# Rational FFN after bucketed attention: both parts of the quotient made on the vector engine

## The chip, the cores and the metric

The kernel runs on one core of one Trainium2 chip. The time is device microseconds of one execution; the run of before was made three times: 946.79, 947.19 and 948.58 us, median 947.19 us. The profile is that of one more execution, which took 947.28 us.

## The reference

An attention over 32 heads of 768 positions, in which a query sees only the keys of its own hash bucket, is followed by a feed-forward layer with a rational activation. Only the second part is touched by the change:

```python
def _moe_ref(x, w_in, w_out, a, b):          # x: 3072 x 512, d_ff 2048
    h = x @ w_in
    h2 = h * h
    h3 = h2 * h
    P = a[0] + a[1] * h + a[2] * h2 + a[3] * h3
    Q = 1.0 + np.abs(b[0]) * np.abs(h) + np.abs(b[1]) * h2
    g = P / (Q + 1e-06)
    return (g @ w_out).astype(np.float32)
```

All of it is float32.

## The kernel before

The attention takes the first 400 us or so. The FFN works on blocks of 384 tokens (8 of them, number t) and chunks of 128 of the 2048 hidden features (16, number f), so on 128 steps (t, f), counted through as i = 0 to 127. The kernel calls TensorE PE, the vector engine DVE, ScalarE ACT and GpSimd POOL, as the profile does.

Float32 products are made from parts: a number is split into a high part in the format fp32r (tiles xh, wi_hi, gh) and the remainder (xl, wi_lo, gl), and three products of parts are summed. So a step has twelve matmuls for h (`Gemm1`, line 581; tile psh; 4 chunks of 128 input features times 3 products) and nine for the output sum (`gemm2`, line 680; tile pso; 3 groups of 128 tokens times 3 products: gh twice, gl once).

`Ffn.step(i)` (line 696) writes the order of the work by hand; each engine keeps its instructions in program order. In one call:

- the first product of step i, and `terms(i)` (line 647): three ACT operations (square, |b0 h|, a3 h + a2) and three on DVE. They leave w = Q - 1 and c, the numerator without a0, in tile `w` (3 buffers) and tile `c1` (3 buffers; the profile shows it as c);
- `quotient(i-1)` (line 660): ACT makes r = 1/Q as exp(-ln Q); DVE makes w = (w + 1.000001) r, then c = (c + a0) r, then c = (w - 2) c. The last two factors are a Newton step on the reciprocal; the result is -g. Tile `r` has 2 buffers;
- `parts(i-2)` (line 673): ACT copies -g to gh, rounded to fp32r, and POOL subtracts: gl = -g - gh. Both have 4 buffers;
- `gemm2(i-4)`: the LAG of 4 steps (line 634) lies between a chunk's first product and its use in the second. At f = 15 ACT copies the three sums out with the factor -1, and they are stored.

During block t the next block's tokens are loaded (`Tokens.load`, line 607). In each of the first 7 blocks this puts four operations of 128 x 768 on DVE (two products x, two remainders xl) and two on ACT, after the steps f = 6, 7, 8 and 12, 13, 14. At i = 6 DVE also makes the last reciprocals of the attention (`recips`). The product of a step lies in one of four PSUM buffers, so PE can be at most four first products ahead of DVE's last reader.

All instructions are issued through a helper, so the profile gives them all as line L88; the tiles tell them apart.

Of the kernel before, what the change touches and what calls it, by code (L numbers as in the profile page):

```python
# [7 lines left out]
F32 = mybir.dt.float32  # L8
F32R = mybir.dt.float32r
# [3 lines left out]
AF = mybir.ActivationFunctionType  # L13
ALU = mybir.AluOpType
# [616 lines left out]
class Ffn:  # L631
# [28 lines left out]
    def quotient(self, t, f):  # L660

        nc = self.nc
        a0, a1, a2, a3, b0, absb1, qbias = self.coef
        w, p = self.state[t, f]
        r = self.tile("r", t, f)
        nc.scalar.activation(r, w, AF.Ln, bias=qbias)
        nc.scalar.activation(r, r, AF.Exp, scale=-1.0)
        nc.vector.scalar_tensor_tensor(out=w, in0=w, scalar=1.0 + 1e-6, in1=r, op0=ALU.add, op1=ALU.mult)
        nc.vector.scalar_tensor_tensor(out=p, in0=p, scalar=a0, in1=r, op0=ALU.add, op1=ALU.mult)
        nc.vector.scalar_tensor_tensor(out=p, in0=w, scalar=2.0, in1=p, op0=ALU.subtract, op1=ALU.mult)  # L670
        self.state[t, f] = p

    def parts(self, t, f):
        p = self.state[t, f]
        gh, gl = self.tile("gh", t, f, 4, F32R), self.tile("gl", t, f, 4, F32R)
        self.nc.scalar.copy(gh, p)
        self.nc.gpsimd.tensor_tensor(out=gl, in0=p, in1=gh.bitcast(F32), op=ALU.subtract)
        self.state[t, f] = gh, gl

    def gemm2(self, t, f):  # L680
        nc = self.nc
        gh, gl = self.state.pop((t, f))
        for i in range(NTK // P):
            if f == 0:
                self.sums[t, i] = self.ps_o.tile([P, DM], F32, tag="pso", name=f"pso{t}_{i}")
            ps = self.sums[t, i]
            ts = slice(i * P, i * P + P)
            for n, (g, w) in enumerate(((gh, 0), (gh, 1), (gl, 0))):
                nc.tensor.matmul(ps, g[:, ts], self.wo[f][:, w, :], start=(f == 0 and n == 0), stop=(f == NFC - 1 and n == 2))
            if f == NFC - 1:  # L690
                o = self.tp.tile([P, DM], F32, tag="o", name=f"o{t}_{i}", bufs=3)
                nc.scalar.activation(o, ps, AF.Identity, scale=-1.0)
                r0 = t * NTK + i * P
                nc.sync.dma_start(self.out[r0 : r0 + P, :], o)

    def step(self, i):
        seq = [(t, f) for t in range(NBLK) for f in range(NFC)]
        if i < len(seq):
            self.gemm(*seq[i])
            self.terms(*seq[i])  # L700
        if 0 <= i - 1 < len(seq):
            self.quotient(*seq[i - 1])
        if 0 <= i - 2 < len(seq):
            self.parts(*seq[i - 2])
        if i >= self.LAG:
            self.gemm2(*seq[i - self.LAG])
        self.done = i + 1
# [70 lines left out]
```

## Time and profile before

| | us |
|---|---|
| median of the three runs | 947.19 |
| the profiled execution | 947.28 |
| its span, from the first to the last instruction | 945.5 |
| PE busy in the span | 937.1 |
| DVE busy | 863.1 |
| ACT busy | 679.7 |
| POOL busy | 454.7 |

How it is read: the page gives each engine's busy time and a strip of 40 slices; the groups of instructions give the mean duration of each kind; the waits name who waited for whom; the timeline gives every instruction's start and duration. Instructions of one engine overlap by some 0.08 us in the records when the second does not need the result of the first: the next one starts before the one ahead has ended. So the sum of durations is more than the time taken, and what an operation takes of DVE's time is read as the distance from its start to the next start.

### The profile page before, as it was taken

The page shows a single profiled execution, that of the slowest core. Times are in us where ns is not written, and L with a number is a line of the kernel's source. Part 1 is how long each engine was busy: PE and PEld are TensorE (multiplying, and loading weights), DVE is VectorE, ACT ScalarE, POOL GpSimd, SP SyncE. Part 2 cuts the span into 40 slices and gives each one's busy share as a digit, 9 for nine tenths or more (in the row PEclk, how much of TensorE's full clock was granted, in tenths as well). Part 3 has the DMA queues.
Part 4 walks back from the last instruction along what each step waited for, and adds up shares of the span by engine and source line. Part 5 has one row for each costly group of instructions (what it writes and reads, how often), then busy time and mean ns, then how long its engine had stood idle before and what let it go on. Part 6 is the DMA issues. An engine that isn't in the chain of part 4 may idle for free.

```text
span 945.5 us, 14855 instructions
## 1 busy us (share of the span) xinstructions
PE 937.1 (99%) x5062; PEld 750.6 (79%) x5062; DVE 863.1 (91%) x1206; ACT 679.7 (72%) x1420; POOL 454.7 (48%) x403
## 2 busy tenths in 40 slices
PE   8999999999999999999999999999999999999998
PEld 4666666666666666589989999899899899998996
DVE  6799889888988896599999999999999999999996
ACT  7577767676767666787777777777777777777775
POOL 5587878787878777832222222222222222222222
PEclk9999999999999999999999999999999999999999
DMA  6677877788777767357021011021010110210000
GB/s 212 193 197 211 235 213 234 215 222 224 233 217 229 220 192 219 117 205 246 6 68 34 1 67 35 1 67 35 32 48 22 63 39 1 67 34 1 34 1 34
DMA packets 49888, 111.65 MB, mean 118 GB/s; under 512 B 9138, under 2 KB 21798, under 8 KB 49812
## 3 DMA queue, kind: packets, MB, share of 16 engines
q1 hardware_dynamic: 49524, 110.60, 39.6%
q8 instruction: 40, 0.66, 0.3%
q14 instruction: 36, 0.29, 0.1%
q10 hardware_dynamic: 288, 0.10, 0.0%
HBM read 56.82 MB, written 21.17 MB: 82 GB/s over the span
## 4 chain that ended last, share of the span: by engine, by line
PE 92%; DVE 5%; DMA 1%; issue 1%; ACT 0%; SPq 0%; DVEq 0%; ACTq 0%
PE psh L88 28%; PE pso L88 28%; PE pss L88 14%; PE psv L88 12%; PE psm L88 6%; DVE m L88 3%; PE psu L88 2%; PE psb L88 1%; DVE ws L88 1%; DMA wr<-w_in 1%; DMA kf<-kT 0%; DVE c L88 0%; DVE wr L88 0%; DVE lo L88 0%; DVE rd L88 0%
## 5 line engine op out<-in xcount | busy, mean ns | idle before, releaser
L88 POOL TENSOR_TENSOR gl<-c,gh 128x384 fp32r<-128x384 f32 x128 | 141.4, 1105 | 393.4 <-ACT gh L88 369.4
L88 ACT ACTIVATE E<-pss 128x384 f32<-128x384 f32 x384 | 167.8, 492 | 112.0 <-PE pss L88 97.5
L88 PE MATMUL pso<-wo,gh 128*128 128x512 f32 x768 | 241.1, 395 | 0.0
L88 DVE TENSOR_REDUCE m<-psm 128x1 f32<-128x768 f32 x192 | 179.4, 948 | 34.6 <-PE psm L88 31.4
L88 POOL TENSOR_TENSOR acc<-E,E 128x384 f32<-128x384 f32 x128 | 160.6, 1273 | 85.7 <-ACT E L88 85.4
L88 PE MATMUL pss<-q,k 128*128 128x384 f32 (+2 forms) x768 | 172.8, 348 | 1.1 <-ACT E L88 0.7
L88 PE MATMUL psh<-xl,wi_hi 128*128 128x384 f32 x512 | 172.1, 336 | 0.0
L88 PE MATMUL psh<-xh,wi_hi 128*128 128x384 f32 x512 | 171.7, 335 | 0.0
L88 PE MATMUL psh<-xh,wi_lo 128*128 128x384 f32 x512 | 171.5, 335 | 0.0
L88 PEld LDWEIGHTS pso<-wo,gh 128*128 128x128 f32 x768 | 142.9, 188 | 23.8
L88 PEld LDWEIGHTS pss<-q,k 128*128 128x128 f32 (+2 forms) x768 | 133.9, 189 | 33.2 <-issue 20.1
L88 PE MATMUL pso<-wo,gl 128*128 128x512 f32 x384 | 152.1, 396 | 0.3 <-POOL gl L88 0.3
L88 ACT ACTIVATE h<-psh 128x384 f32<-128x384 f32 x128 | 63.0, 492 | 123.2 <-PE psh L88 123.2
L88 DVE SCALAR_TENSOR_TENSOR c<-c,ab,r 128x384 f32<-128x384 f32 x128 | 145.9, 1140 | 0.0
L88 POOL TENSOR_TENSOR acc<-acc,E 128x384 f32<-128x384 f32 x128 | 142.6, 1133 | 2.3 <-ACT E L88 2.3
L88 PE MATMUL psv<-E,v 128*64 128x385 f32 x768 | 133.0, 492 | 0.0
L88 PE MATMUL psm<-k,q 76*128 76x384 f32 (+1 forms) x384 | 102.1, 349 | 2.0 <-DVE m L88 1.0
L88 PEld LDWEIGHTS psv<-E,v 128*64 128x64 f32 x768 | 51.9, 136 | 65.0 <-issue 63.7
L88 PEld LDWEIGHTS psh<-xh,wi_hi 128*128 128x128 f32 x512 | 96.1, 188 | 6.3 <-issue 1.2
L88 PEld LDWEIGHTS psh<-xl,wi_hi 128*128 128x128 f32 x512 | 96.0, 188 | 5.1
L88 PEld LDWEIGHTS psh<-xh,wi_lo 128*128 128x128 f32 x512 | 96.1, 188 | 0.0
L88 ACT ACTIVATE c<-psh,ab 128x384 f32<-128x384 f32 x128 | 86.7, 677 | 1.6 <-POOL gl L88 1.4
(77 smaller groups left out, 1284.5 us busy)
## 6 DMA issues: line engine op xcount, KB each, us to landing
q<-q SPq DMA_DIRECT2D x45, 192.0 KB
k<-k SPq DMA_DIRECT2D x45, 192.0 KB
wr<-w_in SPq DMA_DIRECT2D x16, 512.0 KB
wr<-w_out SPq DMA_DIRECT2D x16, 512.0 KB
wo_d<-wr SPq DMA_DIRECT2D x16, 512.0 KB
wo<-wo_d SPq DMA_DIRECT2D x16, 512.0 KB
qf<-qT SPq DMA_DIRECT2D x16, 384.0 KB
kf<-kT SPq DMA_DIRECT2D x16, 384.0 KB
```

The lines of the kernel that those rows point to most:

```text
L88: return self.tc.keep_in_program_order(issue(*args, **kwargs))
```

## The change

The quotient's high part is now DVE's own product gh = (c + a0) r, written as fp32r. The rest of the division is formed from it: w = (w + 1.000001) gh, that is Q times gh, then c = (c + a0) - w, and the low part is gl = c r. `parts` is gone, and with it ACT's copy and POOL's subtraction; DVE has four operations in `quotient` where it had three. The sign is now that of g, so the output copy has no factor.

```diff
         r = self.tile("r", t, f)
+        gh, gl = self.tile("gh", t, f, 4, F32R), self.tile("gl", t, f, 4, F32R)
         nc.scalar.activation(r, w, AF.Ln, bias=qbias)
         nc.scalar.activation(r, r, AF.Exp, scale=-1.0)
-        nc.vector.scalar_tensor_tensor(out=w, in0=w, scalar=1.0 + 1e-6, in1=r, op0=ALU.add, op1=ALU.mult)
-        nc.vector.scalar_tensor_tensor(out=p, in0=p, scalar=a0, in1=r, op0=ALU.add, op1=ALU.mult)
-        nc.vector.scalar_tensor_tensor(out=p, in0=w, scalar=2.0, in1=p, op0=ALU.subtract, op1=ALU.mult)
-        self.state[t, f] = p
-
-    def parts(self, t, f):
-        p = self.state[t, f]
-        gh, gl = self.tile("gh", t, f, 4, F32R), self.tile("gl", t, f, 4, F32R)
-        self.nc.scalar.copy(gh, p)
-        self.nc.gpsimd.tensor_tensor(out=gl, in0=p, in1=gh.bitcast(F32), op=ALU.subtract)
+        nc.vector.scalar_tensor_tensor(out=gh, in0=p, scalar=a0, in1=r, op0=ALU.add, op1=ALU.mult)
+        nc.vector.scalar_tensor_tensor(out=w, in0=w, scalar=1.0 + 1e-6, in1=gh.bitcast(F32), op0=ALU.add, op1=ALU.mult)
+        nc.vector.scalar_tensor_tensor(out=p, in0=p, scalar=a0, in1=w, op0=ALU.add, op1=ALU.subtract)
+        nc.vector.tensor_tensor(out=gl, in0=p, in1=r, op=ALU.mult)
         self.state[t, f] = gh, gl
...
-                nc.scalar.activation(o, ps, AF.Identity, scale=-1.0)
+                nc.scalar.copy(o, ps)
...
-        if 0 <= i - 2 < len(seq):
-            self.parts(*seq[i - 2])
```

What this does to DVE's queue, in the rows of the built programs: c is the numerator tile, psh the first product in PSUM, ab the coefficients, h the square; the first number behind a name is f, and the brackets name the engines whose semaphores the instruction waits for. Before, quotient of step 4 and then the terms of step 6:

```order
L88 SCALAR_TENSOR_TENSOR w_4_4886<-w_4_4886,r_4_4939 128x384 [waits Activation_49]
L88 SCALAR_TENSOR_TENSOR c_4_4887<-c_4_4887,ab,r_4_4939 128x384
L88 SCALAR_TENSOR_TENSOR c_4_4887<-w_4_4886,c_4_4887 128x384 [waits DVE_49]
L88 SCALAR_TENSOR_TENSOR w_6_4973<-h_6_4972,absb_85,w_6_4973 128x384 [waits Activation_49]
L88 TENSOR_TENSOR c_6_4974<-psh_6_4959,c_6_4974 128x384 [waits Activation_49]
L88 SCALAR_TENSOR_TENSOR c_6_4974<-c_6_4974,ab,psh_6_4959 128x384 [waits DVE_49]
```

After, the same place of DVE's queue:

```order
L88 SCALAR_TENSOR_TENSOR gh_4_4940<-c_4_4888,ab,r_4_4939 128x384 [waits PE_49,Activation_49]
L88 SCALAR_TENSOR_TENSOR w_4_4887<-w_4_4887,gh_4_4940 128x384 [waits DVE_49]
L88 SCALAR_TENSOR_TENSOR c_4_4888<-c_4_4888,ab,w_4_4887 128x384 [waits DVE_49]
L88 TENSOR_TENSOR gl_4_4941<-c_4_4888,r_4_4939 128x384 [waits DVE_49,PE_49]
L88 SCALAR_TENSOR_TENSOR w_6_4972<-h_6_4971,absb_85,w_6_4972 128x384 [waits Activation_49]
L88 TENSOR_TENSOR c_6_4973<-psh_6_4958,c_6_4973 128x384 [waits Activation_49]
L88 SCALAR_TENSOR_TENSOR c_6_4973<-c_6_4973,ab,psh_6_4958 128x384 [waits DVE_49]
```

Three of the four operations now wait for the operation right ahead of them on the same engine (DVE_49), where one of three did; and gh and gl each carry a second wait, for PE's last reading of the buffer that they write (from f = 4 of the first block on, 124 steps). In the built program an instruction holds one wait; the first of two stands in an instruction of its own ahead, which does nothing but wait.

## The prediction

> **What bounds the kernel now.** I read the page first, then the waits from 480 us on, then windows, and last the timeline of DVE. The busy shares of the page and its strip for DVE (40 slices of the span):
>
> ```profile
> PE 937.1 (99%) x5062; PEld 750.6 (79%) x5062; DVE 863.1 (91%) x1206; ACT 679.7 (72%) x1420; POOL 454.7 (48%) x403
> DVE  6799889888988896599999999999999999999996
> ```
>
> PE is busy all the time, but in the FFN (the right half of the strip) DVE shows nines as well. The waits after 480 us, as who waited for whom, us in total, times, longest, and the windows of the FFN:
>
> ```profile
> ACT h L88 <- PE psh L88: 103.1, 93, 1.2
> PE pso L88 <- POOL gl L88: 0.3, 1, 0.3
> 404.00:560.00 156.00, 156.00 (x797) 140.55 (x796) 150.91 (x243) 120.04 (x242) 40.93 (x37) 1.00 0.28 95
> 560.00:760.00 200.00, 200.00 (x1004) 180.67 (x1003) 195.63 (x299) 149.14 (x302) 53.63 (x48) 1.00 0.12 36
> ```
>
> PE (the second number of a window) has no gap, at a granted clock of 1.00; its only wait is 0.3 us at the very end. ACT waits for PE. So PE bounds the FFN, and its step is read from ACT's square of the product, once per step; between these two rows lie 55 steps:
>
> ```profile
> 700.01 0.49 ACT L88 ACTIVATE h<-psh 128x384 f32<-128x384 f32 x1 [0.47 <-PE psh L88]
> 930.64 0.49 ACT L88 ACTIVATE h<-psh 128x384 f32<-128x384 f32 x1 [1.21 <-PE psh L88]
> ```
>
> That is 230.63 / 55 = 4.19 us per step. Taking work off ACT and POOL can therefore gain only the 0.3 us at the end. What matters is DVE, of which the change asks more. How much of its 4.19 us does it need? Start, duration, operation:
>
> ```profile
> 708.67 0.61 DVE L88 SCALAR_TENSOR_TENSOR c<-c,ab,r 128x384 f32<-128x384 f32 x1
> 709.32 0.56 DVE L88 SCALAR_TENSOR_TENSOR c<-w,c 128x384 f32<-128x384 f32 x1
> 709.79 0.61 DVE L88 SCALAR_TENSOR_TENSOR w<-h,absb,w 128x384 f32<-128x384 f32 x1
> 710.32 0.55 DVE L88 TENSOR_TENSOR c<-psh,c 128x384 f32<-128x384 f32 x1
> 710.91 0.61 DVE L88 SCALAR_TENSOR_TENSOR c<-c,ab,psh 128x384 f32<-128x384 f32 x1
> 711.44 0.55 DVE L88 SCALAR_TENSOR_TENSOR w<-w,r 128x384 f32<-128x384 f32 x1
> 711.91 1.38 DVE L88 SCALAR_TENSOR_TENSOR c<-c,ab,r 128x384 f32<-128x384 f32 x1
> 713.32 0.56 DVE L88 SCALAR_TENSOR_TENSOR c<-w,c 128x384 f32<-128x384 f32 x1
> 711.52 1.35 POOL L88 TENSOR_TENSOR gl<-c,gh 128x384 fp32r<-128x384 f32 x1 [3.18 <-ACT gh L88]
> ```
>
> From start to start, the terms take 0.53, 0.59 and 0.53 (709.79 to 711.44, 1.65), the quotient 0.47 (711.44 to 711.91), 0.65 (708.67 to 709.32) and 0.47 (709.32 to 709.79): 3.24 us. The operation that lies beside POOL's subtraction took 1.38 where its like took 0.61: it ends 0.42 after POOL does, as if it had been held. So 0.76 of DVE's "busy" time is waiting behind POOL, and DVE has room of almost 1 us per step. Two kinds of distance stand here. Where the next operation does not need the result, it starts 0.08 before the end (709.32 + 0.56 = 709.88, next at 709.79). Where it does (708.67 + 0.61 = 709.28, next at 709.32; 710.32 + 0.55 = 710.87, next at 710.91), it starts 0.04 behind the end. A dependence thus costs some 0.12.
>
> **The change part by part.** Gone: ACT's copy, POOL's subtraction, and with POOL the hold.
>
> ```profile
> L88 ACT CAST gh<-c 128x384 fp32r<-128x384 f32 x91 | 45.3, 498 | 0.0
> L88 DVE TENSOR_TENSOR x<-x,r 128x768 f32<-128x768 f32 x11 | 10.5, 951 | 0.0
> L88 DVE TENSOR_TENSOR xl<-x,xh 128x768 fp32r<-128x768 f32 x11 | 10.5, 951 | 0.0
> ```
>
> The copy's 0.50 us on ACT lay beside PE, which ACT waits for anyway: worth nothing. That gh is written as fp32r costs DVE nothing: xl and x take the same 951 ns. The output copy without its factor stays on ACT, three times per block beside PE: taken as nothing, at most a tenth of its time once, at the end.
>
> DVE's quotient, each operation waiting for the one ahead: gh 0.64 to 0.65, as its like above (0.61 and 0.04; I take 0.64, which the one quoted further down has); w, with a constant instead of a column, 0.55 + 0.04 = 0.59; c again 0.64; gl is followed by an operation that does not need it, 0.47 (as c<-w,c; 0.53 if it is like the forms with a column). Sum 2.34. With the terms 3.99 us per step, without the second waits.
>
> The second wait of gl is the unknown. Its first wait, for DVE's own result, moves into an instruction of its own, so behind the end of c come two steps instead of one. Before has such a pair on DVE, at the end of the attention:
>
> ```order
> L88 SCALAR_TENSOR_TENSOR ws_4637<-ws_4637,wr_4636 128x512 [waits DVE_49]
> L88 ISA ws_4637<-wr_4636,ws_4637 128x1024 [waits DVE_49,Activation_49]
> L88 TENSOR_TENSOR wr_4636<-ws_4637,wr_4636 128x512 [waits Activation_49]
> L88 SCALAR_TENSOR_TENSOR w_0_4711<-h_0_4710,absb_85,w_0_4711 128x384 [waits PE_49,Activation_49]
> L88 TENSOR_TENSOR c_0_4712<-psh_0_4697,c_0_4712 128x384 [waits Activation_49]
> ```
>
> The second row is that operation; ISA there is the custom operation of the profile. ACT has one in the last step, whose copy to gh waits for DVE and PE, while the copy before it waits for DVE alone:
>
> ```profile
> 401.48 1.37 DVE L88 SCALAR_TENSOR_TENSOR ws<-ws,wr 128x512 int32<-128x512 int32 x1
> 402.98 1.28 DVE L88 CUSTOM_DVE_ANT_0 ws<-wr,ws 128x1024 uint16<-128x1024 uint16 x1
> 410.14 0.61 DVE L88 SCALAR_TENSOR_TENSOR c<-c,ab,r 128x384 f32<-128x384 f32 x1
> 410.78 0.56 DVE L88 SCALAR_TENSOR_TENSOR c<-w,c 128x384 f32<-128x384 f32 x1
> 935.23 0.56 DVE L88 SCALAR_TENSOR_TENSOR c<-w,c 128x384 f32<-128x384 f32 x1
> 935.82 0.51 ACT L88 CAST gh<-c 128x384 fp32r<-128x384 f32 x1 [1.12 <-DVE c L88]
> 936.82 1.25 DVE L88 SCALAR_TENSOR_TENSOR c<-w,c 128x384 f32<-128x384 f32 x1
> 938.16 0.51 ACT L88 CAST gh<-c 128x384 fp32r<-128x384 f32 x1 [1.82 <-DVE c L88]
> ```
>
> On DVE 402.98 - 402.85 = 0.13 behind the end, against 0.03 with one wait (410.78 - 410.75): 0.10 more, but the operation is a custom one. On ACT 0.09 (938.16 - 938.07) against 0.03: 0.06 more. I take 0.07, nearer to the plain operation, with 0 and 0.10 as ends. The second wait of gh I take at nothing: gh does not need the operation right ahead of it, so its wait for PE, long over, is passed while that one runs; 0.06 if it isn't. What is queued behind gl on DVE is the next step's terms, and for those wait ACT's ln and then PE, four steps on.
>
> Now the sum. The steps i = 0 to 3 have no second products yet (the LAG), so PE takes about half a step's time for each of them and DVE falls behind at once; with 3.99 + 0.07 per step and the tokens (0.87 four times per block of 16) it needs 4.28 where PE needs 4.19, and cannot catch up. So DVE has no idle time, and its own work sets the end. The rows for the start, the reciprocals at i = 6, and a remainder with the operation behind it:
>
> ```profile
> 405.90 0.62 DVE L88 SCALAR_TENSOR_TENSOR w<-h,absb,w 128x384 f32<-128x384 f32 x1 [0.25 <-ACT w L88]
> 407.98 0.62 DVE L88 SCALAR_TENSOR_TENSOR w<-h,absb,w 128x384 f32<-128x384 f32 x1 [0.31 <-ACT w L88]
> 429.40 0.18 DVE L88 TENSOR_SCALAR rz<-rs 128x48 f32<-128x48 f32 x1
> 430.56 0.90 DVE L88 TENSOR_TENSOR x<-x,r 128x768 f32<-128x768 f32 x1
> 705.41 0.95 DVE L88 TENSOR_TENSOR xl<-x,xh 128x768 fp32r<-128x768 f32 x1
> 706.27 0.61 DVE L88 SCALAR_TENSOR_TENSOR w<-h,absb,w 128x384 f32<-128x384 f32 x1
> ```
>
> 405.90 start; 0.43 idle until 407.98 (behind terms of 1.65); 128 x 1.65 = 211.2; 128 x 2.34 = 299.5; 124 x 0.07 = 8.7; 28 token operations x 0.87 = 24.4 (705.41 to 706.27, with 0.95 - 0.08); reciprocals 1.16. DVE is through at 951.3, and gl's own end is 0.08 later, 951.4. Behind it PE has seven of the last step's nine matmuls. The end of before:
>
> ```profile
> 937.71 0.50 PE L88 MATMUL pso<-wo,gl 128*128 128x512 f32 x1 [0.32 <-POOL gl L88]
> 941.38 0.40 PE L88 MATMUL pso<-wo,gl 128*128 128x512 f32 x1
> ```
>
> From the one to the end of the other lie 16 matmuls, 4.07 us, so seven take 1.78: 953.2. From the last matmul's end to the end of the span there were 945.5 - 941.78 = 3.72 us: 956.9, or 11.4 more than the 945.5 now. On the profiled 947.28 this is 958.7; that execution lies 0.1 over the median, so 947.19 + 11.4 = **958.6 us**.
>
> The point from which it decides: gl of the last step must be there by 941.78 - 1.78 = 940.0, so DVE may take (940.0 - 0.1 - 405.9 - 0.4 - 24.4 - 1.2) / 128 = 3.97 us per step, waits and all. My 3.99 + 0.07 is 2% over it, and all 128 steps pay.
>
> **The rivals.**
>
> *The second wait is free* (the sequencer passes both at once): 8.7 less, 949.9 us, +0.3%. For it: the operation's other wait is long over. Against it: both pairs of rows above.
>
> *DVE keeps up, and nothing changes or a little is gained.* If a wait cost nothing and only the pipe's flow counted, the operations would follow each other at 0.53 (four with a column) and 0.47 (three without): 3.53 us per step, far under 3.97; PE would stay the bound, and without its 0.3 us wait the time is 946.9. The mechanism is that of the rows at 709.32 and 709.79. Against it are the rows at 708.67 and 709.32 in the same step: the dependent one comes 0.04 behind the end. [...]
>
> *gh's second wait shows too*, at ACT's 0.06 in 124 steps: 7.4 more, 966.0. Against it: the operation ahead of gh runs 0.61, time enough to pass a wait that is over. With gl's at the custom operation's 0.10 alone it would be 3.7 more, 962.3, which I count with the forecast.
>
> **How the numbers follow.** Forecast 0.72 (DVE bound, second wait of gl between 0.05 and 0.10, each step good to 0.02, which is 2.5 us: 954 to 963); free wait 0.10; DVE keeps up 0.08; gh's wait shows too 0.10. The range from 949.5 to 963 holds the first two, 0.82. A measurement here can tell some 0.2% from no change, 1.9 us, so 945.3 to 949.1 is "same". Slower: forecast, free wait and gh's wait, less a little of the free wait that may fall under 949.1: 0.90. Of the 0.08, most is same, 0.07, and faster 0.03 allows for a gain that I don't see.
>
> **What would show it.** Right: in the timeline of DVE no idle time in the FFN; c<-c,ab,r and w<-w,r never beyond 0.65; behind c some 0.10 to gl; a step from 4.06 us without tokens; PE waiting for gl by DVE, some 11 us in all, most of it in blocks 2 to 7 and a few us in the last steps, where PE has only second products left and DVE is still more than two steps behind. Wrong: DVE waiting for ACT's w in every step (then it has room), PE without waits, or a distance from c to gl like that from gh to w.

## The result, and the profile after

The changed kernel takes 963.8 us (median of 4 runs, 962.5 to 964.5) against 947.4 us (4 runs) for the kernel before: a ratio of 1.0164, 95% interval 1.0149 to 1.0179. It is slower by 16 us. The profiled execution took 962.49 us with a span of 960.7 us, 15.2 us more than the span of before.

The busy shares of the page, the strip of DVE, and the waits from 404 us on (who waited for whom, us in total, times, longest):

```profile
PE 939.5 (98%) x5062; PEld 751.8 (78%) x5062; DVE 863.4 (90%) x1334; ACT 630.0 (66%) x1292; POOL 313.3 (33%) x275
DVE  6799888879888996699999999999999999999996
```

```profile
ACT h L88 <- PE psh L88: 168.8, 112, 5.3
ACT xh L88 <- DVE x L88: 17.4, 13, 4.4
PEld psh L88 <- DVE xl L88: 15.3, 7, 5.7
PE psh L88 <- DVE xl L88: 13.0, 7, 5.4
```

The strip of DVE is the same nines in the FFN as before, and its busy time is the same 863 us. The share does not tell the two kernels apart: before, it was filled up with waiting behind POOL, now with work. What is new is in the waits: PE waits for DVE, 13.0 us. It waits for xl, the low part of the next block's tokens, seven times, once near the head of each of the blocks 2 to 8.

DVE in the middle of a block, start and duration:

```profile
700.22 0.61 DVE L88 SCALAR_TENSOR_TENSOR w<-h,absb,w 128x384 f32<-128x384 f32 x1
700.75 0.55 DVE L88 TENSOR_TENSOR c<-psh,c 128x384 f32<-128x384 f32 x1
701.34 0.61 DVE L88 SCALAR_TENSOR_TENSOR c<-c,ab,psh 128x384 f32<-128x384 f32 x1
701.87 0.61 DVE L88 SCALAR_TENSOR_TENSOR gh<-c,ab,r 128x384 fp32r<-128x384 f32 x1
702.51 0.56 DVE L88 SCALAR_TENSOR_TENSOR w<-w,gh 128x384 f32<-128x384 f32 x1
703.11 0.62 DVE L88 SCALAR_TENSOR_TENSOR c<-c,ab,w 128x384 f32<-128x384 f32 x1
703.83 0.56 DVE L88 TENSOR_TENSOR gl<-c,r 128x384 fp32r<-128x384 f32 x1
704.31 0.61 DVE L88 SCALAR_TENSOR_TENSOR w<-h,absb,w 128x384 f32<-128x384 f32 x1
```

The hold by POOL is gone: no operation of 128 x 384 is longer than 0.62. From start to start the step is 0.53, 0.59, 0.53 for the terms and 0.64, 0.60, 0.72, 0.48 for the quotient: 4.09 us (700.22 to 704.31), where the kernel before needed 3.24 beside its hold. The 0.72 is the place where gl waits for c through an instruction of its own: 0.10 of DVE's time lie between the end of c (703.73) and gl. The groups of instructions show it as idle time, the last column; for comparison a group with one wait for the operation right ahead stands beside it:

```profile
L88 DVE SCALAR_TENSOR_TENSOR w<-h,absb,w 128x384 f32<-128x384 f32 x128 | 78.3, 612 | 0.6 <-ACT w L88 0.6
L88 DVE TENSOR_TENSOR gl<-c,r 128x384 fp32r<-128x384 f32 x128 | 71.5, 558 | 13.0
L88 DVE SCALAR_TENSOR_TENSOR c<-c,ab,w 128x384 f32<-128x384 f32 x128 | 79.2, 619 | 4.6
```

DVE waits 0.6 us for ACT in all the FFN, at its first two steps; 13.0 / 128 is the 0.10 ahead of each gl, and 4.6 / 128 the 0.04 behind another dependence. Apart from these short gaps DVE works without a pause from its second step to its last.

Its pace is that of the kernel. The second xl of a block, in two blocks one behind the other, is made here at

```profile
606.00 0.95 DVE L88 TENSOR_TENSOR xl<-x,xh 128x768 fp32r<-128x768 f32 x1
674.84 0.95 DVE L88 TENSOR_TENSOR xl<-x,xh 128x768 fp32r<-128x768 f32 x1
```

and in the kernel before at

```profile
596.38 0.95 DVE L88 TENSOR_TENSOR xl<-x,xh 128x768 fp32r<-128x768 f32 x1
663.47 0.95 DVE L88 TENSOR_TENSOR xl<-x,xh 128x768 fp32r<-128x768 f32 x1
```

A block now takes 68.84 us, where it took 67.09 at PE's pace; 16 steps of 4.09 and four token operations of 0.87 are 68.9. Without the token operations DVE's step, 4.09, would be shorter than PE's 4.19: it takes them on top to put DVE behind, block by block. PE at the head of the second block, and of the fourth:

```profile
463.40 0.34 PE L88 MATMUL psh<-xh,wi_hi 128*128 128x384 f32 x1
469.12 0.69 PE L88 MATMUL psh<-xl,wi_hi 128*128 128x384 f32 x1 [5.38 <-DVE xl L88]
469.61 0.52 PE L88 MATMUL psh<-xh,wi_lo 128*128 128x384 f32 x1
469.93 0.52 PE L88 MATMUL psh<-xh,wi_hi 128*128 128x384 f32 x1
...
605.21 0.34 PE L88 MATMUL psh<-xh,wi_hi 128*128 128x384 f32 x1
607.01 0.45 PE L88 MATMUL psh<-xl,wi_hi 128*128 128x384 f32 x1 [1.47 <-DVE xl L88]
607.30 0.34 PE L88 MATMUL psh<-xh,wi_lo 128*128 128x384 f32 x1
607.47 0.33 PE L88 MATMUL psh<-xh,wi_hi 128*128 128x384 f32 x1
```

PE makes seven of the new block's first twelve matmuls, the last of them (at 463.40 and 605.21) with the high part of the second half of the input features, and then waits for the low part of that half, which is the xl made at f = 14: 5.38 us the first time, at most 1.5 later. Behind the long wait the matmuls come 0.32 apart, behind the short one 0.17. The end, DVE's last operation and PE's last matmul:

```profile
953.61 0.56 DVE L88 TENSOR_TENSOR gl<-c,r 128x384 fp32r<-128x384 f32 x1
956.50 0.40 PE L88 MATMUL pso<-wo,gl 128*128 128x512 f32 x1
```

DVE is through at 954.17, and PE begins the nine matmuls of the last step after that, at 954.62; PE ends at 956.90, 15.1 us later than before (941.78), and 3.8 us later the span ends.

### The profile page after: what moved, and what is told of

It is laid out like the page before. It is cut to its first block, busy times and chain, and to the rows that moved or that the text cites. A ratio compares the mean times of both kernels' runs of the same rounds, so it can differ in the third digit from the quotient of the medians.

```text
span 960.7 us, 14845 instructions
## 1 busy us (share of the span) xinstructions
PE 939.5 (98%) x5062; PEld 751.8 (78%) x5062; DVE 863.4 (90%) x1334; ACT 630.0 (66%) x1292; POOL 313.3 (33%) x275
## 4 chain that ended last, share of the span: by engine, by line
PE 69%; DVE 23%; issue 4%; DMA 2%; ACT 1%; SPq 1%; DVEq 0%; ACTq 0%
PE psh L88 16%; PE pso L88 16%; PE pss L88 14%; PE psv L88 12%; PE psm L88 6%; DVE c L88 6%; DVE w L88 5%; DVE gh L88 3%; DVE gl L88 2%; DVE m L88 2%; PE psu L88 2%; PE psb L88 1%; DVE x L88 1%; DMA s_d<-sr 1%; DVE xl L88 1%
## 5 line engine op out<-in xcount | busy, mean ns | idle before, releaser
L88 PEld LDWEIGHTS pso<-wo,gl 128*128 128x128 f32 x384 | 72.7, 189 | 17.8
L88 DVE SCALAR_TENSOR_TENSOR c<-c,ab,w 128x384 f32<-128x384 f32 x128 | 79.2, 619 | 4.6
```

The costliest lines, as they stand in the source:

```text
L88: return self.tc.keep_in_program_order(issue(*args, **kwargs))
```

## The experiments

Two theories stood at the start. One: DVE's work sets the time, whatever PE happens to wait for. The other: the waits for xl are a matter of when xl is made, two steps ahead of its use. All ratios are against the kernel before on the same chip.

**One wait less for gl** (e1_gl5).

```diff
-        gh, gl = self.tile("gh", t, f, 4, F32R), self.tile("gl", t, f, 4, F32R)
+        gh, gl = self.tile("gh", t, f, 4, F32R), self.tile("gl", t, f, 5, F32R)
```

> gl gets a fifth buffer, so that its wait for PE is covered by gh's and only the wait for DVE is left, in gl itself; nothing else changes. Theory (DVE's work sets the time): the distance from c to gl falls from 0.72 to 0.65, DVE needs 124 x 0.07 = 8.7 us less, its last gl ends near 945.5 instead of 954.2, and the time falls by 7 to 9 us, to about 956. Rival (the 13 us are a matter of when xl is made, two steps ahead of its use, and the wait instruction lies beside other work): the distance falls or not, the time stays at 963 to 964.

Measured: 956.8 us, ratio 1.0090 (1.0074 to 1.0107). DVE around gl, its last operation, and PE's waits:

```profile
703.76 0.62 DVE L88 SCALAR_TENSOR_TENSOR c<-c,ab,w 128x384 f32<-128x384 f32 x1
704.41 0.56 DVE L88 TENSOR_TENSOR gl<-c,r 128x384 fp32r<-128x384 f32 x1
...
947.15 0.56 DVE L88 TENSOR_TENSOR gl<-c,r 128x384 fp32r<-128x384 f32 x1
```

```profile
PE psh L88 <- DVE xl L88: 6.4, 6, 4.7
```

The distance from c to gl is 0.65 instead of 0.72, and 0.07 in 124 steps is worth 7 us of kernel. PE's waits for xl fall with it, from 13.0 to 6.4 us. A second wait that has long been met is not free if it turns the first one into an instruction of its own behind the very operation that it waits for.

**The tokens earlier** (e3_early).

```diff
-                    if f == 3 + 6 * c:
+                    if f == 3 + 4 * c:
                         coming = tokens.load(t + 1, c)
-                    if f - 3 - 6 * c in (0, 3, 4, 5):
+                    if f - 3 - 4 * c in (0, 2, 3, 4):
                         next(coming)
```

> The next block's token operations are put at f = 3, 5, 6, 7 and 7, 9, 10, 11 instead of 3, 6, 7, 8 and 9, 12, 13, 14: the last xl is made five steps ahead of its use instead of two. DVE's work is the same. Theory (DVE's work sets the time): the waits for xl go, others come in their place (for gl, or in the last steps); DVE is through at 954 as after, the span is at least 954.2 + 1.8 + 3.8 = 959.8, the time 961 to 963. Rival (the margin of xl is the cause): the 13 us of waits and PE's slow start behind the first go, 948 to 950 us.

Measured: 964.2 us, ratio 1.0168 (1.0146 to 1.0190): nothing gained. The waits:

```profile
ACT w L88 <- DVE c L88: 98.6, 83, 1.3
...
PEld pso L88 <- ACT o L88: 11.4, 7, 1.7
PE pso L88 <- ACT o L88: 8.4, 7, 1.3
PEld pso L88 <- DVE gl L88: 7.3, 12, 1.6
```

PE's waits for xl are gone, and others stand there: for gl, and for ACT's copy of the finished sums, which is queued behind ACT's w, which in turn waits for DVE to free its buffer. DVE takes 549.3 us from its first FFN operation (408.02) to its end (957.36), in the changed kernel 548.8 (405.36 to 954.17); only its first FFN operation came 2.7 us later in this execution. (A second profile of the changed kernel, e9_after_again, has the same span as this one, 963.1 us.) So in the changed kernel the place of the wait decides nothing. DVE's work does.

**Both** (e5_gl5_early), the two diffs above together.

> The fifth buffer of e1_gl5 and the early token operations of e3_early together. Theory (DVE's work sets the end, the waits only move): DVE is through as in e1_gl5, near 947.7 in the profile, the span is at least 947.7 + 1.8 + 3.8 = 953.3, the time 954 to 957, no more than 2 us under e1_gl5. Rival (with the second wait gone what is left is the margin of xl): 948 to 950.

Measured: 954.5 us, ratio 1.0062 (1.0043 to 1.0081), 2.4 us under e1_gl5. DVE needs 539.9 us, 8.9 less than in the changed kernel and 2.1 less than in e1_gl5 (542.0, from 405.70 to 947.71). The intervals of the two ratios overlap a little, so that the early tokens gain here is likely but not shown; if they do, it is little. PE's waits for xl are gone, and small ones for ACT's copy and for gl stand in their place.

**The same seven operations in turn** (e2_inter). `terms` and `quotient` issue their ACT part and hand back their DVE operations; `step` issues these alternately.

```diff
-            self.terms(*seq[i])
-        if 0 <= i - 1 < len(seq):
-            self.quotient(*seq[i - 1])
+        ours = self.terms(*seq[i]) if i < len(seq) else []
+        late = self.quotient(*seq[i - 1]) if 0 <= i - 1 < len(seq) else []
+        for n in range(4):
+            for ops in (late, ours):
+                if n < len(ops):
+                    ops[n]()
```

> The same seven DVE operations per step, with the quotient of step i-1 and the terms of step i in turn (gh, w, w, c, c, c, gl), so that no operation needs the one right ahead of it. Theory (a dependence costs 0.12 from start to start, a second wait 0.07 only behind one): distances of 0.47 to 0.53, 3.5 to 3.6 us per step plus 0.22 for the tokens, under PE's 4.19: DVE idles, PE is the bound again, no wait for xl, 946.5 to 948 us. Rival (the next operation waits for an empty pipe in any case, the order makes no difference; what costs is the seventh operation): 963 to 964 as after.

Measured: 948.1 us (10 runs), ratio 0.9997 (0.9987 to 1.0006): the time of before, with all of the change's operations on DVE. The timeline of DVE and a wait of the same kernel:

```profile
702.12 0.62 DVE L88 SCALAR_TENSOR_TENSOR gh<-c,ab,r 128x384 fp32r<-128x384 f32 x1 [0.40 <-ACT r L88]
702.66 0.61 DVE L88 SCALAR_TENSOR_TENSOR w<-h,absb,w 128x384 f32<-128x384 f32 x1
703.19 0.55 DVE L88 SCALAR_TENSOR_TENSOR w<-w,gh 128x384 f32<-128x384 f32 x1
703.66 0.55 DVE L88 TENSOR_TENSOR c<-psh,c 128x384 f32<-128x384 f32 x1
704.12 0.61 DVE L88 SCALAR_TENSOR_TENSOR c<-c,ab,w 128x384 f32<-128x384 f32 x1
704.65 0.61 DVE L88 SCALAR_TENSOR_TENSOR c<-c,ab,psh 128x384 f32<-128x384 f32 x1
705.18 0.55 DVE L88 TENSOR_TENSOR gl<-c,r 128x384 fp32r<-128x384 f32 x1
```

```profile
DVE gh L88 <- ACT r L88: 49.2, 89, 1.9
```

Every operation of these rows starts 0.46 to 0.54 behind the one ahead. Six distances, 702.12 to 705.18, are 3.06 us, and DVE waits 49 us for ACT: it has room, and PE has none of the waits above. The durations in the records are what they were; only the distances shrank. gl has its two waits here too, and it starts 0.53 behind the operation ahead, like the independent ones: another operation stands between it and c. So the rival falls: the order of the same seven operations is worth 16 us, because a wait for the operation right ahead costs 0.12, and one through an instruction of its own 0.19. Four such distances, 4 x 0.12 + 0.07 = 0.55, account for the difference between 4.09 and 3.53 (the 3.06 and 0.47 for gl).

The Trainium skill, "VectorE: DVE Perf Modes", section "The DRAIN you can't avoid", says that the next operation does not start until the pipe is empty and that a semaphore costs nothing extra there; it also says that an operation that is not held starts earlier. The trace agrees with the second: the independent operations here start 0.08 before the recorded end of the one ahead. That a semaphore costs nothing does not hold here for one that waits for the operation right ahead.

**gl on POOL** (e4_pool).

```diff
-        nc.vector.tensor_tensor(out=gl, in0=p, in1=r, op=ALU.mult)
+        nc.gpsimd.tensor_tensor(out=gl, in0=p, in1=r, op=ALU.mult)
```

> The last product of the quotient, gl = c r, is made on POOL; the other three operations stay on DVE. Theory: DVE has six operations, 3.42 us per step plus 0.22 for the tokens; POOL's gl lies beside the terms that read PSUM and holds little; PE is the bound, 946.5 to 948 us. Rival (POOL beside DVE holds it as in the kernel before, 0.76 in each step, on top of the longer chain: 3.42 + 0.76 + 0.22 = 4.40): DVE stays the bound, above 965 us.

Measured: 947.8 us (10 runs), ratio 0.9994 (0.9985 to 1.0003). With six operations DVE has room for POOL's hold: w<-h is the one held, in about half of the steps, up to 1.4 us from start to start, and PE does not wait. (The theory had the right time but placed POOL's gl beside other operations.) So e1_gl5, with 0.07 us off DVE's step, moves the time by 7 us, and e2_inter and this kernel, with more off it, move it down to PE's bound and no further.

**An eighth operation in turn** (e7_inter8).

```diff
             lambda: nc.vector.tensor_tensor(out=gl, in0=p, in1=r, op=ALU.mult),
+            lambda: nc.vector.tensor_tensor(out=spare, in0=r, in1=r, op=ALU.mult),
```

with `spare` a tile of its own, and `range(5)` in `step`.

> The order in turn of e2_inter, with an eighth DVE operation per step behind gl: r times r into a spare tile that nothing reads. Theory (DVE's time counts, not the number of its operations): the distances of e2_inter sum to 3.52 us, with 0.47 for the eighth 3.99 us per step, 0.22 for the tokens; this is 0.02 over the point of 3.97 from which DVE decides, so 1 to 4 us over the kernel before, 949 to 952, and well under the changed kernel, which has an operation less. Rival (one operation too many on DVE is what costs): more than the changed kernel's 964, about 964 + 128 x 0.47 = 1024 if DVE is full as it is there.

Measured: 964.0 us, ratio 1.0158 (1.0141 to 1.0176). Neither theory said so. DVE's eight distances are as expected, 3.99 us, but DVE is not busy throughout; a wait of PE and one of DVE, then DVE's rows:

```profile
PE psh L88 <- DVE xl L88: 12.2, 7, 5.8
...
DVE gh L88 <- ACT r L88: 3.9, 3, 1.9
```

```profile
701.97 0.55 DVE L88 TENSOR_TENSOR spare<-r 128x384 f32<-128x384 f32 x1
702.64 0.62 DVE L88 SCALAR_TENSOR_TENSOR gh<-c,ab,r 128x384 fp32r<-128x384 f32 x1
```

From spare to gh it is 0.67 instead of 0.47: DVE stands still 0.2 us in such a step, waiting for r, which ACT finishes at 702.61. The order in turn begins with gh, which needs the last result of ACT's step, where the terms needed the second; so DVE runs later behind PE, with little room to catch up, and xl, two steps ahead of its use, is late once per block though DVE has idle time. This would be the second theory's mechanism, in a kernel that I had not thought of; that the margin of xl is the cause is what the next run tests.

**The eighth operation with the tokens earlier** (e8_inter8_early), beside the changed kernel once more (e9_after_again).

> The eight operations in turn of e7_inter8 with the early token operations of e3_early. In e7_inter8 a step of DVE took 3.99 as expected, but the time was that of the changed kernel: DVE waited for r and PE for xl once per block. Theory (there xl's margin is the cause, since gh at the head of DVE's step waits for the end of ACT's; DVE's work alone would be through near 944): with the last xl three steps earlier the waits for xl go, nothing comes in their place, 947 to 952 us. Rival (an eighth operation, or DVE's work, is what costs there): 962 or more, as in e3_early, where the same edit moved the waits and gained nothing.

> The changed kernel once more, beside e8_inter8_early on the same chip: 963 to 965 us by every theory; it gives the ratio that e8_inter8_early is held against.

Measured: 951.6 us, ratio 1.0034 (1.0022 to 1.0047), and 964.7 us, ratio 1.0173 (1.0143 to 1.0203), for the changed kernel. The windows of the middle of the FFN (PE busy is the second number) show that PE's gaps are gone there:

```profile
404.00:560.00 156.00, 154.18 (x785) 138.13 (x784) 152.84 (x303) 106.09 (x200) 2.18 (x2) 1.00 0.28 94
560.00:760.00 200.00, 200.00 (x1001) 180.04 (x1000) 200.00 (x394) 135.17 (x255) 0.00 (x0) 1.00 0.11 34
```

Of the 1.82 us without PE in the first window, 1.64 are one wait for ACT's copy of the first block's sums; another wait lies near the end:

```profile
485.95 0.50 PE L88 MATMUL pso<-wo,gh 128*128 128x512 f32 x1 [1.64 <-ACT o L88]
944.82 0.50 PE L88 MATMUL pso<-wo,gl 128*128 128x512 f32 x1 [0.53 <-DVE gl L88]
```

So something did come in place of the waits for xl, but little. Eight operations on DVE, one of them for nothing, are 13 us quicker than the changed kernel's seven. The same edit of the tokens gains 12 us here and nothing in e3_early: there DVE had no room, here it had room at the wrong time.

No version beat the kernel before: e2_inter and e4_pool have its time to within the measurement, and PE, without waits in both, is the bound.

## Why the prediction was right in kind and short in size

- *PE bounds the kernel before; work taken off ACT and POOL gains nothing*: right. In e2_inter that work is gone too, and the time is that of before.
- *The hold by POOL goes, and DVE's own time decides*: right. DVE has no pause between 408 and 954 us, and 6.8 us less of its work (548.8 to 542.0 in e1_gl5) made the kernel 7.0 us quicker.
- *The price of the operations, 3.99*: a little low. gh to w is 0.64 to 0.65, w to c 0.60 where I had 0.59, gl to the next 0.48 where I had 0.47; without the second wait it is 4.09 - 0.07 = 4.02.
- *The second wait of gl, 0.07 between 0 and 0.10*: right, 0.07 by e1_gl5. That of gh, *at nothing*: right; from the last c to gh it is the 0.53 of before.
- *DVE is through at 951.4*: 954.2. These 2.8 us are the larger part of what was missed in the span: DVE's work took 548.8 us where the sum had 545.5, some 0.026 more in each of 128 steps, and it began earlier by 0.5 (405.36).
- *PE waits for gl, some of it in the last steps*: wrong. It waits for xl near the heads of the blocks, 13.0 us in all. I had counted the token operations as time on DVE and not looked at when their result is needed: xl is made at f = 14 and read in the next block's first product, two steps on, while gl has a LAG of four. For the sum it mattered little, as e3_early shows, where the waits moved and the time stayed.
- *Seven matmuls behind the last gl, 1.78 us*: wrong as a path, and 0.9 us short: it was 2.73 (954.17 to 956.90). PE never waited for gl at all. It had lost its time near the heads of the blocks and was itself behind at the end, with the last step's nine matmuls still to begin when the last gl came; in the last block, without token operations, DVE's 4.09 is the shorter step. So the chain that ended last did not run through the last gl. That the two paths end within 0.9 us of each other is luck: nothing in the prediction foresaw it.
- Together 2.8 + 0.9 + 0.1 at the tail make the 3.8 us between the span foretold, 956.9, and 960.7. The rest, to a median of 963.8 against 958.6, is that the profiled execution lies 1.3 us under its median, where that of before lay 0.1 over it. The measured median lies 0.8 above the upper end that was given, 963; the measured ratio on the 947.19 that the forecast started from is 962.7, just under it.

The rival "the second wait is free" fell with the 0.72; "DVE keeps up", with the 0.60 to 0.72 that dependent operations take from start to start; "gh's second wait shows too", with the 0.53. The times of two cases that did not happen, 962.3 for a second wait of 0.10 and 966.0 for gh's, lie nearer to the measured 963.8 than the forecast's 958.6 does: a near number does not make a mechanism right.

## What to carry to other kernels

A busy share near full says nothing about room: take the distances from start to start where nothing holds the engine, add the whole step, and compare it with the step of the engine that bounds. On DVE order the operations so that none needs the one right ahead; two independent chains in turn do it, and there an added operation takes only its own 0.47 us of DVE's time (e7_inter8). When an engine loses its room, look at every result that it makes and ask how many steps ahead of its use it is made; the shortest distance shows the wait first, but only an experiment tells whether moving it gains anything or only moves the wait.

## What the runs showed of the hardware

- Behind an idle time of 5.38 us PE ran at half its rate: 0.32 from matmul to matmul (469.61 to 469.93) instead of 0.17, until 472.08. That is 3 us from the first of them, at 469.12, and cost another 1.5 us or so (an estimate, half of these 3 us). The window around it has a granted clock of 0.84 (the number behind POOL's busy time):

```profile
462.00:473.00 11.00, 5.62 (x22) 4.82 (x21) 10.41 (x19) 5.68 (x12) 0.00 (x0) 0.84 0.00 0
```

  e1_gl5 shows the same behind 4.7 us, and e7_inter8 behind 5.8, there for 4.3 us (470.57 to 474.90). Waits of 1.64 us (e8_inter8_early, at 485.95) and less leave the rate alone: behind them the next first products come 0.17 to 0.18 apart. The Trainium skill, "TensorE: Matmul & The Clock Gate", section "Part 1: The HAM clock gate (the "warmup" mystery)", tells of a clock that is halved behind some 3.4 us of idling and comes back after as long at work. The traces agree as far as they go: idle times of 4.7 us and more slowed PE, those of 1.64 and less did not, and the slow stretches lasted 3.0 to 4.3 us.
- In the kernel before, an operation of DVE that reads two step tensors from SBUF (w, c, r, h) and starts while POOL's gl runs ends 0.41 to 0.43 us after gl does, in all 127 cases; c<-c,ab,r takes 1.37 to 1.40 then instead of 0.61. Of those that read the product in PSUM, c<-c,ab,psh starts beside a running gl 20 times and takes its 0.61 each time:

```profile
420.32 1.02 POOL L88 TENSOR_TENSOR gl<-c,gh 128x384 fp32r<-128x384 f32 x1 [2.25 <-ACT gh L88]
420.64 0.61 DVE L88 SCALAR_TENSOR_TENSOR c<-c,ab,psh 128x384 f32<-128x384 f32 x1
```

  In e4_pool the operation that meets gl is w<-h, one of the first kind.
